# First four token blocks of a fused attention + gMLP kernel: loads re-split over two queues, a hand-set order on DVE and ACT

## The chip, the cores and the metric

One core of a Trainium2 chip. Times are device microseconds (us) of one execution; a lower time is better. "Span" is the time from the first to the last instruction in the profile; the device time is 1.7 to 2.5 us longer in nearly all runs here, in two clusters near 1.8 and 2.3, so for effects below a microsecond I compare spans as well. PE is TensorE, DVE is VectorE, ACT is ScalarE, POOL is GpSimd, SP is SyncE (which only issues transfers here).

## The reference

Two branches on the same layer-normed input, added to the residual (2048 tokens, width 512):

```python
xn = layernorm(x)                                   # 2048 x 512
A  = dilated_local_attention(xn @ wqkv) @ wo        # 32 heads, 8 keys, dilation 2
z  = gelu(xn @ w_in)                                # 2048 x 1792
z1, z2 = z[..., :896], layernorm(z[..., 896:])
B  = (z1 * (w_sp @ z2 + b_sp)) @ w_out              # w_sp is 2048 x 2048
return x + A + B
```

The tokens come in 16 blocks of 128. Block 0 to 3 must be loaded, normed and transposed before PE has any real work; the change is about them.

## The kernel before

The kernel is written as a list of tasks with reads, writes and estimated durations. A list scheduler turns them into one order per engine, and waits are put in from the dependencies. The order on PE is mostly the order of the code; on DVE, ACT and POOL the scheduler picks by its estimates. The loads at the start, in issue order:

```python
for h in range(2):                       # x block 0 in halves: x0a on SP, x0b on ACT
    dma(("sp", "act")[h], ... x2[0:128, 256*h : 256*h+256] ...)
ld_x(1, "sp")                            # x block 1, 128 KB
ld_win_h("w_in2a", FH, HF)               # first column half of z2's weights: 224 KB on each queue
ld_x(2, "sp")
ld_x(3, "act")
ld_win_h("w_in2b", FH + HF, HF)          # second column half: 224 KB on each queue
for which, eng in ((0, "sp"), (1, "act")):   # wq on SP, wk on ACT, 512 KB each
    ...
```

A block is normed with statistics on DVE, the power -0.5 on POOL, subtract and multiply on DVE, transposes on PE, an evacuation on ACT (block 0 half on ACT, half on DVE). Then z2 needs two half blocks of four matmuls each; the first half needs w_in2a only, the second w_in2b. Much later, at the end of the z2 stage, ACT alternates squares and gelus:

```python
def z2_n(j):
    for b in range(4 * j, 4 * j + 4):
        if b == NB - 2:
            z1_block(0)                  # four+four matmuls into two PSUM banks, then a gelu on ACT
        z2_sq(b)                         # square with row sum, on ACT
    z2_wave(j)
...
for b in range(1, NB):
    z1_block(b)
```

## Time and profile before

| | before |
|---|---|
| device time, median of the first 3 runs | 235.09 us (234.59 to 235.51) |
| span of the profiled run | 233.1 us |
| PE busy | 227.4 us, 98% |
| PE waits up to 217 us, once PE has real work | 0.86 us for w_in, 0.3 us for ACT at z1 |

The table of stretches of the kernel before, cut at the points where PE changes its work. Columns: start and end, length, then the busy time of PE, of its weight loads, of DVE, ACT and POOL with their instruction counts, the granted clock, the DMA share and GB/s:

```profile
5.19:8.26 3.07, 2.13 (x14) 0.95 (x15) 2.45 (x7) 1.43 (x4) 0.93 (x2) 1.00 1.04 353
8.26:14.37 6.11, 6.09 (x37) 3.30 (x38) 3.68 (x11) 4.75 (x15) 4.20 (x21) 1.00 1.05 339
80.46:107.37 26.91, 26.62 (x162) 14.93 (x160) 26.37 (x28) 17.90 (x25) 1.03 (x1) 1.00 0.25 52
107.37:217.60 110.23, 110.23 (x566) 55.21 (x565) 105.94 (x91) 45.37 (x76) 0.00 (x0) 1.00 0.85 196
```

The reader is to see that PE shows as idle for 0.94 us in the first stretch, 0.29 in the third (z1), and not at all in the 110 us of products after it. The change aims at the first and the third.

### The profile page before, as it was taken

To read this page: it belongs to the slowest core of one execution; us is meant where nothing else is said; L and a number is where in the kernel's file an instruction comes from. 1 tells how busy PE (TensorE), PEld (TensorE's weight loads), DVE (VectorE), ACT (ScalarE), POOL (GpSimd) and SP (SyncE) were. 2 spreads that over 40 slices of the span, in tenths; PEclk is the share of its full clock that TensorE was granted. 3 is DMA by queue.
4 is the path that set the end of the run, shared out by engine and by line. 5 is a ranking of instruction groups with operands and counts; after the bars stand their busy time and mean duration, and the time that the engine had idled before them with its cause. 6 is when DMAs were issued, how large, how long until landed. Compare 5 with 4: busy or idle time off the path is not lost.

```text
span 233.1 us, 3309 instructions
## 1 busy us (share of the span) xinstructions
PE 227.4 (98%) x1238; PEld 111.6 (48%) x1238; DVE 205.3 (88%) x238; ACT 129.4 (56%) x235; POOL 44.3 (19%) x74
## 2 busy tenths in 40 slices
PE   7899999999999999999999999999999999999995
PEld 2444444444444556555555554544544545545443
DVE  4688799989988899999999999999999999979910
ACT  3598768968889996556563243333423433255211
POOL 4455859257343101000000000000000000000000
PEclk9999999999999999999999999999999999999999
DMA  6997998941007200359709999999999747744082
GB/s 196 355 217 151 292 192 246 328 106 68 25 0 177 93 3 0 67 113 199 233 19 183 224 210 282 246 232 291 232 333 115 174 157 146 251 111 103 23 174 65
DMA packets 77456, 38.65 MB, mean 166 GB/s; under 512 B 65148, under 2 KB 75900, under 8 KB 76416
## 3 DMA queue, kind: packets, MB, share of 16 engines
q1 hardware_dynamic: 70272, 31.17, 58.9%
q10 hardware_dynamic: 6352, 5.15, 7.2%
q0 software_dynamic: 816, 2.12, 2.7%
q8 instruction: 10, 0.16, 0.3%
q14 instruction: 6, 0.05, 0.1%
HBM read 18.49 MB, written 4.21 MB: 97 GB/s over the span
## 4 chain that ended last, share of the span: by engine, by line
PE 88%; DMA 4%; ACT 3%; DVE 2%; SPq 1%; issue 0%; DVEq 0%
PE ps L1099 36%; PE ps L1218 13%; PE ps L757 12%; PE ps L886 10%; PE ps L904 8%; PE ps L737 6%; PE ps L796 3%; DMA arena<-in_B_w_in_dram 2%; DMA arena<-arena 2%; ACT arena L915 2%; ACT arena L910 1%; DVE arena L1176 1%; DVE arena L1116 1%; SPq L1179 1%; DVE arena L1132 0%; SPq L604 0%
## 5 line engine op out<-in xcount | busy, mean ns | idle before, releaser
L1099 PE MATMUL ps<-arena 128*128 128x448 bf16 x448 | 90.6, 352 | 0.0
L1099 PEld LDWEIGHTS ps<-arena 128*128 128x128 bf16 x448 | 43.8, 98 | 42.8 <-ACT arena L1055 0.3
L1218 PE MATMUL ps<-arena 128*128 128x512 bf16 (+2 forms) x187 | 44.1, 367 | 0.2 <-DMA arena<-arena 0.2
L1167 DVE TENSOR_TENSOR arena<-arena 128x4096 bf16<-128x4096 bf16 x16 | 36.6, 2286 | 0.3
L783 DVE TENSOR_TENSOR arena<-arena 128x4096 bf16<-128x4096 bf16 x16 | 36.0, 2280 | 0.0
L1176 DVE TENSOR_TENSOR arena<-arena 128x4096 bf16<-128x4096 bf16 (+2 forms) x24 | 33.6, 1401 | 1.1 <-DMA arena<-arena 0.4
L1055 ACT ACTIVATE arena<-ps 128x512 bf16<-128x512 f32 (+2 forms) x23 | 13.0, 564 | 34.8 <-PE ps L1099 23.8
L757 PE MATMUL ps<-arena 128*128 128x512 bf16 x128 | 28.5, 379 | 0.0
L1218 PEld LDWEIGHTS ps<-arena 128*128 128x128 bf16 x187 | 17.9, 98 | 18.9 <-DMA arena<-arena 0.5
L886 PE MATMUL ps<-arena 128*128 128x448 bf16 x128 | 25.7, 353 | 1.0 <-DMA arena<-in_B_w_in_dram 0.9
L904 PE MATMUL ps<-arena 128*128 128x448 bf16 x128 | 25.0, 353 | 0.3 <-ACT arena L910 0.3
L990 DVE TENSOR_TENSOR arena<-arena 128x1024 bf16<-128x1024 bf16 x32 | 21.1, 686 | 1.2 <-DMA arena<-in_B_w_sp_dram 0.9
L891 ACT ACTIVATE arena<-ps 128x448 bf16<-128x448 f32 x32 | 17.3, 546 | 5.1 <-PE ps L886 3.1
L757 PEld LDWEIGHTS ps<-arena 128*128 128x128 bf16 x128 | 12.4, 98 | 15.4 <-ACT arena L891 0.4
L765 ACT ACTIVATE arena<-ps 128x1024 bf16<-128x1024 f32 x16 | 16.3, 1020 | 5.8 <-PE ps L757 5.7
L904 PEld LDWEIGHTS ps<-arena 128*128 128x128 bf16 x128 | 14.3, 114 | 10.8 <-issue 0.8
L910 ACT ACTIVATE arena<-ps 128x896 bf16<-128x896 f32 x16 | 14.4, 914 | 8.9 <-PE ps L904 8.9
L886 PEld LDWEIGHTS ps<-arena 128*128 128x128 bf16 x128 | 12.1, 98 | 13.4 <-DMA arena<-in_B_w_in_dram 1.0
L771 POOL COPY arena<-arena 128x16 bf16<-128x16 bf16 x12 | 13.8, 1149 | 7.9 <-ACT arena L765 7.9
L915 ACT ACTIVATE arena<-arena 128x896 bf16<-128x896 bf16 x16 | 15.1, 944 | 0.2
L737 PE MATMUL ps<-arena 128*128 128x512 bf16 x64 | 14.5, 379 | 0.0
L1108 ACT ACTIVATE ps<-ps,fpool 128x448 f32<-128x448 f32 x16 | 9.7, 604 | 8.1 <-PE ps L1099 8.1
(74 smaller groups left out, 195.0 us busy)
## 6 DMA issues: line engine op xcount, KB each, us to landing
arena<-vscr SPq DMA_DIRECT2D x8, 1152.0 KB, 6.5
arena<-in_A_x_dram ACTq DMA_DIRECT2D x17, 128.0 KB, 3.9
vscr<-arena POOLq DMA_DIRECT2D x16, 128.0 KB, 2.9
arena<-in_A_x_dram SPq DMA_DIRECT2D x14, 128.0 KB, 6.2
out_dram<-arena ACTq DMA_DIRECT2D x14, 128.0 KB, 2.7
arena<-in_A_wqkv_dram SPq DMA_DIRECT2D x2, 512.0 KB, 7.8
arena<-in_B_w_in_dram SPq DMA_DIRECT2D x1, 896.0 KB, 6.0
arena<-in_B_w_out_dram SPq DMA_DIRECT2D x1, 896.0 KB, 5.7
```

What stands on the lines that cost most here:

```text
L737: last = t.matmul(bank(k), AC(off["xnT"] + dc * S + 128 * b, [[1, 128]]), AC(off["wv_raw"] + 512 * dc, [[1, 512]]), start=(dc == 0), stop= ...
L757: last = t.matmul(bank(k + which), AC(off["wqk"] + 1024 * dc + col0, [[1, 128]]), AC(off["xnT"] + dc * S + 512 * j, [[1, 512]]), start=(dc ...
L783: T("dve", lambda v: v.tensor_tensor(pbv, qb, kb, ALU.mult), reads=rd, writes=[("pb", s_)], est=c_dve(4096, 2.0), name="prod%d_%d" % (j, c ...
L886: last = t.matmul(ps[:, 512 * k: 512 * k + HF], AC(off["xnT"] + dc * S + 128 * b, [[1, 128]]), AC(off["w_in2"] + FH * dc + c0, [[1, HF]]), ...
L891: T("act", (lambda k, hf: lambda a: a.activation(A("z2", HF, FH * b + HF * hf), ps[:, 512 * k: 512 * k + HF], ACTF.Gelu_apprx_tanh, accum_ ...
L904: last = t.matmul(ps[:, 512 * (k + hf): 512 * (k + hf) + HF], AC(off["xnT"] + dc * S + t0, [[ts, 128]]), AC(off["w_in1"] + FH * dc + HF * ...
L915: T("act", lambda a: a.activation(A("sqj", FH), A("z2", FH, FH * b), ACTF.Square, accum_out=Fv("s2", 1, b)), reads=[("z2h", b, 0), ("z2h", ...
L990: T("dve", (lambda o_, x_, y_: lambda v: v.tensor_tensor(o_, x_, y_, ALU.subtract))(o_, x_, y_), reads=rd, writes=[wr], est=c_dve(NK * 128 ...
L1099: last = t.matmul(half(bk), lh(k), rh(k), start=(new and k == 0), stop=(k == NK - 1), skip_group_check=True)
L1167: T("dve", (lambda tv, iv, av: lambda v: v.tensor_tensor(tv, iv, av, ALU.mult))(tv, iv, av), reads=[("attn", j)] + ([("Ve", par)] if q < 2 ...
L1176: T("dve", (lambda o_, n: lambda v: v.tensor_tensor(o_, two(0, n), two(n, n), ALU.add))(o_, n), reads=[] if n > 512 else ["Vs", ("Ve", par ...
L1218: last = t.matmul(po, lh, rh, start=False, stop=(q == len(order) - 1), skip_group_check=True)
```

## The change

The intent: get w_in's second half to PE sooner, with the first two blocks of x in front in small pieces; have no engine do anything in the first 14 us but what PE waits for next; and, later, give PE a free bank pair sooner in the z1 stage. The diff, cut to its core (cuts are marked with dots; the comments on the order are mine):

```diff
-        for h in range(2):
-            dma(("sp", "act")[h], ... x2[0:128, 256 * h: 256 * h + 256] ...)
-        ld_x(1, "sp")
+        for b in range(2):
+            for h in range(2):
+                dma(("sp", "act")[h], ... x2[128 * b: 128 * b + 128, 256 * h: 256 * h + 256] ...)
         ld_win_h("w_in2a", FH, HF)
         ld_x(2, "sp")
+        ld_win_h("w_in2b", FH + HF, HF)
         ld_x(3, "act")
-        ld_win_h("w_in2b", FH + HF, HF)
-        for which, eng in ((0, "sp"), (1, "act")):
+        for which, eng in ((0, "sp"), (1, "sp")):
 ...
+            plan.sequence(dv)            # DVE: stats 0a 0b, aggr 0, stats 1a 1b, norm 0a 0b, aggr 1, evacuate 0b,
+                                         #   stats 2a, norm 1, stats 2b, aggr 2, stats 3, aggr 3, norm 2, norm 3
+            names = ["xTe0", "xTe1", "z2g0_0", "xTe2", "z2g0_1", "z2g1_0", "xTe3", "z2g1_1"]   # ACT
+            plan.sequence([named[n] for n in names])
 ...
         def z2_n(j):
-                if b == NB - 2:
-                    z1_block(0)
+                if b >= NB - 2:
+                    z1_block(b - NB + 2)
                 z2_sq(b)
 ...
-        for b in range(1, NB):
+        for b in range(2, NB):
             z1_block(b)
 ...
+        by_name["QKe3_3"].odeps.add(by_name["sexp1"])    # last evacuation of Q, K after the first exp
+        by_name["eV0_0"].odeps.add(by_name["sexp3"])     # first V evacuation of the products after the second exp
```

More of the change, by code (lines that the diff above doesn't have):

```diff
@@ L390, in build_kernel @@
     for name, n in (("mx", 128), ("Zb", 256), ("Z", 128), ("maskt", 128 if True else 256), ("st6", NB * 9),
-                    ("mv", NB * 2), ("st0", 15), ("rstd", NB), ("s1", 2 * NB), ("s2", NB), ("m2", NB), ("msq", NB),
+                    ("mv", NB * 2), ("st0", 45), ("rstd", NB), ("s1", 2 * NB), ("s2", NB), ("m2", NB), ("msq", NB),
                     ("vpe2", NB), ("rstd2", NB), ("mhalf", 4), ("bia", NB), ("bdf", NB // 2)):
@@ L462, in build_kernel @@
             if s_ < 2:
-                R1(("xin0", s_), "xin", 256, 256 * s_)
+                for h in range(2):
+                    R1(("xinh", s_, h), "xin", 256, 512 * s_ + 256 * h)
                 R1(("xn0", s_), "xn", 256, 256 * s_)
@@ L550, in build_kernel @@
           name="steps1")
-        T("dve", lambda v: v.memset(Fv("st0", 2, 12), 0.0), writes=["st0e"], est=160, name="steps2")
-        T("dve", lambda v: v.memset(Fv("st0", 1, 14), LN_EPS * D), writes=["st0e"], est=160, name="steps3")
+        T("dve", lambda v: v.memset(FCa(foff["st0"] + 12, [[15, 3], [1, 2]]), 0.0), writes=["st0e"], est=160, name="steps2")
+        T("dve", lambda v: v.memset(FCa(foff["st0"] + 14, [[15, 3], [1, 1]]), LN_EPS * D), writes=["st0e"], est=160, name="steps3")
         T("pool", lambda g: g.memset(mhalf, -0.5), writes=["mhalf"], est=110, name="mhalf")
@@ L617, in ld_win_h @@
                     256 * n * 2, (nm, h), writes=[(nm, h)], name="ld%s_%d" % (nm, h))
-        for h in range(2):
-            dma(("sp", "act")[h], (lambda h: lambda e: e.dma_start(A("xin", 256, 256 * h), x2[0:128, 256 * h: 256 * h + 256]))(h),
-                128 * 256 * 2, ("xin0", h), writes=[("xin0", h)], name="ldx0%s" % "ab"[h])
-        ld_x(1, "sp")
+        for b in range(2):
+            for h in range(2):
+                dma(("sp", "act")[h], (lambda b, h: lambda e: e.dma_start(
+                    A("xin", 256, 512 * b + 256 * h), x2[128 * b: 128 * b + 128, 256 * h: 256 * h + 256]))(b, h),
+                    128 * 256 * 2, ("xinh", b, h), writes=[("xinh", b, h)], name="ldx%d%s" % (b, "ab"[h]))
         ld_win_h("w_in2a", FH, HF)
         ld_x(2, "sp")
+        ld_win_h("w_in2b", FH + HF, HF)
         ld_x(3, "act")
-        ld_win_h("w_in2b", FH + HF, HF)
-        for which, eng in ((0, "sp"), (1, "act")):
+        for which, eng in ((0, "sp"), (1, "sp")):
             dma(eng, (lambda which: lambda e: e.dma_start(
@@ L664, in next_pair, with first_wave, bn, ag @@
             return k
-        def ln_first():
-            for h in range(2):
-                T("dve", (lambda h: lambda v: v.bn_stats(Fv("st0", 6, 6 * h), A("xin", 256, 256 * h)))(h),
-                  reads=[("xin0", h)], writes=[("st0", h)], est=420, name="bnst0%s" % "ab"[h])
-            T("dve", lambda v: v.bn_aggr(Fv("mv", 2), Fv("st0", 15)), reads=[("st0", 0), ("st0", 1), "st0e"],
-              writes=[("mv", 0)], est=180, name="bnag0")
-            T("pool", lambda g: g.tensor_tensor(Fv("rstd", 1), Fv("mv", 1, 1), Fv("mhalf", 1), ALU.pow),
-              reads=[("mv", 0), "mhalf"], writes=[("rstd", 0)], est=580, name="rstd0")
-            ks = (next_bank(), next_bank())
-            for h in range(2):
-                T("dve", (lambda h: lambda v: v.tensor_scalar(A("xn", 256, 256 * h), A("xin", 256, 256 * h), Fv("mv", 1),
-                                                              Fv("rstd", 1), ALU.subtract, ALU.mult))(h),
-                  reads=[("xin0", h), ("mv", 0), ("rstd", 0)], writes=[("xn0", h)], est=270, name="norm0%s" % "ab"[h])
-                def tr(t, h=h):
+        def first_wave():
+            dv = []
+            def bn(b, h):
+                dv.append(T("dve", lambda v: v.bn_stats(Fv("st0", 6, 15 * b + 6 * h), A("xin", 256, 512 * b + 256 * h)),
+                            reads=[("xinh", b, h) if b < 2 else ("xin", b)], writes=[("st0", b, h)], est=370,
+                            name="bnst%d%s" % (b, "ab"[h])))
+            def ag(b):
+                dv.append(T("dve", lambda v: v.bn_aggr(Fv("mv", 2, 2 * b), Fv("st0", 15, 15 * b) if b < 3 else Fv("st6", 9, 9 * b)),
+                            reads=[("st0", b, 0), ("st0", b, 1), "st0e"] if b < 3 else [("st6", b), "st_eps"],
+                            writes=[("mv", b)], est=200, name="bnag%d" % b))
+                T("pool", lambda g: g.tensor_tensor(Fv("rstd", 1, b), Fv("mv", 1, 2 * b + 1), Fv("mhalf", 1), ALU.pow),
+                  reads=[("mv", b), "mhalf"], writes=[("rstd", b)], est=580, name="rstd%d" % b)
+            def nm(b, c0=0, n=512, wr=None, tag=""):
+                dv.append(T("dve", lambda v: v.tensor_scalar(A("xn", n, 512 * b + c0), A("xin", n, 512 * b + c0), Fv("mv", 1, 2 * b),
+                                                             Fv("rstd", 1, b), ALU.subtract, ALU.mult),
+                            reads=[("xinh", b, h) for h in range(2)] + [("xin", b), ("mv", b), ("rstd", b)],
+                            writes=[wr or ("xn", b)], est=150 + n / 2, name="norm%d%s" % (b, tag)))
+            def xt(b, k, dcs, rd, tag=""):
+                def tr(t):
@@ L681, in tr @@
                     last = None
-                    for dc in (2 * h, 2 * h + 1):
-                        last = t.matmul(ps[:, 512 * ks[h] + 128 * dc: 512 * ks[h] + 128 * dc + 128],
-                                        A("xn", 128, 128 * dc), ident, start=True, stop=True)
-                    return last
-                T("pe", tr, reads=[("xn0", h), "ident"], writes=[("ps", ks[h])], est=2 * c_mm(128), name="xTr0%s" % "ab"[h])
+                    for dc in dcs:
+                        last = t.matmul(ps[:, 512 * k + 128 * dc: 512 * k + 128 * dc + 128],
+                                        A("xn", 128, 512 * b + 128 * dc), ident, start=True, stop=True)
@@ new lines, in tr, with ev @@
+                    return last
+                T("pe", tr, reads=[rd, "ident"], writes=[("ps", k)], est=len(dcs) * c_mm(128), name="xt%d%s" % (b, tag))
+            def ev(b, k):
+                T("act", lambda a: a.activation(AC(off["xnT"] + 128 * b, [[S, 4], [1, 128]]),
+                                                bank(k).rearrange("p (c n) -> p c n", c=4), ACTF.Copy),
+                  reads=[("ps", k)], writes=[("xnT", b)], est=c_act(512), name="xTe%d" % b)
+            bn(0, 0)
+            bn(0, 1)
@@ L687, in ln_first @@
+            ag(0)
+            bn(1, 0)
+            bn(1, 1)
+            k0, k1 = next_bank(), next_bank()
+            nm(0, 0, 256, ("xn0", 0), "a")
+            xt(0, k0, (0, 1), ("xn0", 0), "a")
             T("act", lambda a: a.activation(AC(off["xnT"], [[S, 2], [1, 128]]),
-                                            ps[:, 512 * ks[0]: 512 * ks[0] + 256].rearrange("p (c n) -> p c n", c=2),
+                                            ps[:, 512 * k0: 512 * k0 + 256].rearrange("p (c n) -> p c n", c=2),
@@ L689, in ln_first @@
                                             ACTF.Copy),
-              reads=[("ps", ks[0])], writes=["xnT0a"], est=c_act(256), name="xTe0")
-            T("dve", lambda v: v.tensor_copy(AC(off["xnT"] + 2 * S, [[S, 2], [1, 128]]),
-                                             ps[:, 512 * ks[1] + 256: 512 * ks[1] + 512].rearrange("p (c n) -> p c n", c=2)),
-              reads=[("ps", ks[1])], writes=["xnT0b"], est=c_dve(256), name="xTf0")
-            filler(cfg["fill0"], "fill0", 216.0 * cfg["fill0"], reads=("zeros", ("xn0", 1)))
+              reads=[("ps", k0)], writes=["xnT0a"], est=c_act(256), name="xTe0")
@@ new lines, in first_wave @@
+            nm(0, 256, 256, ("xn0", 1), "b")
+            xt(0, k1, (2, 3), ("xn0", 1), "b")
+            ag(1)
+            dv.append(T("dve", lambda v: v.tensor_copy(AC(off["xnT"] + 2 * S, [[S, 2], [1, 128]]),
+                                                       ps[:, 512 * k1 + 256: 512 * k1 + 512].rearrange("p (c n) -> p c n", c=2)),
+                        reads=[("ps", k1)], writes=["xnT0b"], est=c_dve(256), name="xTf0"))
+            filler(cfg["fill0"], "fill0", 216.0 * cfg["fill0"], reads=("zeros", ("xn0", 1)))
@@ new lines, in first_wave @@
+            z2_half(0, 0)
+            bn(2, 0)
+            nm(1)
+            k = next_bank()
+            xt(1, k, range(4), ("xn", 1))
+            ev(1, k)
+            bn(2, 1)
+            ag(2)
+            z2_half(0, 1)
+            dv.append(T("dve", lambda v: v.bn_stats(Fv("st6", 6, 27), A("xin", 512, 1536)), reads=[("xin", 3)],
+                        writes=[("st6", 3)], est=690, name="bnst3"))
+            ag(3)
+            nm(2)
+            z2_half(1, 0)
+            k = next_bank()
@@ new lines, in first_wave @@
+            xt(2, k, range(4), ("xn", 2))
+            ev(2, k)
+            z2_half(1, 1)
+            nm(3)
+            k = next_bank()
+            xt(3, k, range(4), ("xn", 3))
+            ev(3, k)
+            z2_half(2, 0)
+            z2_half(2, 1)
+            z2_half(3, 0)
+            z2_half(3, 1)
+            plan.sequence(dv)
+            names = ["xTe0", "xTe1", "z2g0_0", "xTe2", "z2g0_1", "z2g1_0", "xTe3", "z2g1_1"]
+            named = {t.name: t for t in plan.tasks if t.name in names}
@@ L696, in ln_block @@
+            plan.sequence([named[n] for n in names])
         def ln_block(b):
-            if b == 0:
-                return ln_first()
             sl = b % 4
@@ L702, in ln_block @@
             T("dve", lambda v: v.bn_stats(Fv("st6", 6, 9 * b), xin),
-              reads=[("xin", xs_)] + (["xnT0b"] if b == 2 else []), writes=[("st6", b)],
+              reads=[("xin", xs_)], writes=[("st6", b)],
               est=690, name="bnst%d" % b)
@@ L711, in ln_block @@
               reads=[("xin", xs_), ("mv", b), ("rstd", b)], writes=[("xn", sl)], est=400, name="norm%d" % b)
-            if b >= XDMA:
-                dma("sp", lambda e: e.dma_start_transpose(AC(off["xnT"] + 128 * b, [[S, 4], [1, 128]]),
-                                                          A("xn", 512, 512 * sl)),
-                    128 * 512 * 2, ("xT", sl), reads=[("xn", sl)], writes=[("xnT", b)], name="xTd%d" % b, xbar=True)
-                return
-            k = next_bank()
-            def tr(t):
-                last = None
-                for dc in range(4):
-                    last = t.matmul(ps[:, 512 * k + 128 * dc: 512 * k + 128 * dc + 128],
-                                    A("xn", 128, 512 * sl + 128 * dc), ident, start=True, stop=True)
-                return last
-            T("pe", tr, reads=[("xn", sl), "ident"], writes=[("ps", k)], est=4 * c_mm(128), name="xTr%d" % b)
-            T("act", lambda a: a.activation(AC(off["xnT"] + 128 * b, [[S, 4], [1, 128]]),
-                                            bank(k).rearrange("p (c n) -> p c n", c=4), ACTF.Copy),
-              reads=[("ps", k)], writes=[("xnT", b)], est=c_act(512), name="xTe%d" % b)
+            dma("sp", lambda e: e.dma_start_transpose(AC(off["xnT"] + 128 * b, [[S, 4], [1, 128]]),
+                                                      A("xn", 512, 512 * sl)),
+                128 * 512 * 2, ("xT", sl), reads=[("xn", sl)], writes=[("xnT", b)], name="xTd%d" % b, xbar=True)
         def v_block(b):
@@ L876, in softmax_tail, with z2_half, mm @@
               reads=[dk, "R"], writes=[("attn", j)], est=c_dve(1024, 2.0), name="sattn%d" % j, prio=FILL)
+        def z2_half(b, hf):
+            k = next_bank()
+            c0 = HF * hf
+            def mm(t):
+                last = None
+                for dc in range(4):
+                    last = t.matmul(ps[:, 512 * k: 512 * k + HF], AC(off["xnT"] + dc * S + 128 * b, [[1, 128]]),
+                                    AC(off["w_in2"] + FH * dc + c0, [[1, HF]]), start=(dc == 0), stop=(dc == 3))
+                return last
+            T("pe", mm, reads=[("xnT", b), (("w_in2a", "w_in2b")[hf], 0), (("w_in2a", "w_in2b")[hf], 1)], writes=[("ps", k)],
+              est=4 * c_mm(HF), name="z2_%d_%d" % (b, hf))
+            T("act", lambda a: a.activation(
+                A("z2", HF, FH * b + HF * hf), ps[:, 512 * k: 512 * k + HF], ACTF.Gelu_apprx_tanh,
+                accum_out=Fv("s1", 1, 2 * b + hf)),
+              reads=[("ps", k)], writes=[("z2h", b, hf), ("s1", b, hf)], est=c_act(HF, accum=True),
+              name="z2g%d_%d" % (b, hf), tbl="gelu")
         def z2_block(b):
             for hf in range(2):
-                k = next_bank()
-                c0 = HF * hf
-                def mm(t, k=k, c0=c0):
-                    last = None
-                    for dc in range(4):
-                        last = t.matmul(ps[:, 512 * k: 512 * k + HF], AC(off["xnT"] + dc * S + 128 * b, [[1, 128]]),
-                                        AC(off["w_in2"] + FH * dc + c0, [[1, HF]]), start=(dc == 0), stop=(dc == 3))
-                    return last
-                T("pe", mm, reads=[("xnT", b), (("w_in2a", "w_in2b")[hf], 0), (("w_in2a", "w_in2b")[hf], 1)], writes=[("ps", k)],
-                  est=4 * c_mm(HF), name="z2_%d_%d" % (b, hf))
-                T("act", (lambda k, hf: lambda a: a.activation(
-                    A("z2", HF, FH * b + HF * hf), ps[:, 512 * k: 512 * k + HF], ACTF.Gelu_apprx_tanh,
-                    accum_out=Fv("s1", 1, 2 * b + hf)))(k, hf),
-                  reads=[("ps", k)], writes=[("z2h", b, hf), ("s1", b, hf)], est=c_act(HF, accum=True),
-                  name="z2g%d_%d" % (b, hf), tbl="gelu")
+                z2_half(b, hf)
         def z1_block(b):
@@ L1020, in v_wave @@
                 v_block(b)
-        ln_wave(0)
+        first_wave()
         setup_masks()
-        z2_w(0)
         qk_wave(0)
@@ L1307, in build_kernel @@
             f_()
+        by_name = {t.name: t for t in plan.tasks}
+        by_name["QKe3_3"].odeps.add(by_name["sexp1"])
+        by_name["eV0_0"].odeps.add(by_name["sexp3"])
         plan.sequence(pe_seq)
```

## The prediction

> **What bounds the kernel now.** I read four views, in this order: the page (shares and slices), the chain that ended last, the table of stretches, and the timeline of the first 15 us. The page comes first because it says whether any engine but TensorE matters:
>
> ```profile
> PE 227.4 (98%) x1238; PEld 111.6 (48%) x1238; DVE 205.3 (88%) x238; ACT 129.4 (56%) x235; POOL 44.3 (19%) x74
> PE 88%; DMA 4%; ACT 3%; DVE 2%; SPq 1%; issue 0%; DVEq 0%
> ```
>
> TensorE (PE) has 5.7 us in the whole 233.1 us span in which it does nothing, and the chain that ended last runs 88% through it. So the change can only win from those 5.7 us, from PE work that is mere filler, or from work moved off PE; it moves none off. The chain in order of time says where it leaves PE:
>
> ```profile
> 2.70 5.52 DMA arena<-in_B_w_in_dram
> 8.22 0.05 issue
> 8.26 1.69 PE ps L886 x8
> ...
> 11.16 3.20 PE ps L886 x16
> 14.37 6.91 PE ps L757 x32
> ...
> 80.50 0.64 ACT arena L891 x2
> ...
> 85.96 0.81 ACT arena L910
> 86.77 0.05 issue
> 86.81 7.76 PE ps L904 x40
> ```
>
> The reader is to see three things. The chain starts with a load of w_in (the second column half's last piece, issued at 2.70, landed at 8.22), from there PE never lets go until 80.48; then comes an ACT (ScalarE) stretch to 86.77; the last exit is the tail after 217.6, which the change does not touch. Now the first stretch on PE itself, from the timeline of PE alone:
>
> ```profile
> 6.25 0.93 PE L886 MATMUL ps<-arena 128*128 128x448 bf16 x4
> 7.02 0.39 PE L722 MATMUL ps<-arena 128*128 128x128 bf16 x4
> 8.26 1.69 PE L886 MATMUL ps<-arena 128*128 128x448 bf16 x8 [0.86 <-DMA arena<-in_B_w_in_dram]
> ```
>
> The first half block of z2 (the gMLP gate input) runs at 6.25, the transposes of block 1 follow, then PE stands 0.86 us until the second half of w_in is there. After it PE is full: in the table of stretches PE is busy 5.92 of 5.94 us from 8.26 to 14.20, and all 30.80 us from there to 45.0. The only other PE wait up to 217 us in the view of waits is 0.3 us on ACT (the evacuation of z1) at 86.8.
>
> **What the Trainium skill says.** "Perfetto Trace Analysis", section "Optimization Strategy": find the gaps on the most contended engine and what blocks there. This trace agrees that this is the way to read it: two gaps in the first 217 us once PE has started on real work, 0.86 and 0.29 us. "DMA: Bandwidth & Descriptors", section "Queues, rings and completion order": each DMA engine takes turns between the queues that have work. The trace agrees: from 3.0 to 8.3 us the SP queue moved 0.16 + 0.14 + 0.14 + 0.18 + 0.24 = 0.86 MB and the ACT queue 0.24 + 0.12 + 0.20 + 0.15 + 0.25 = 0.96 MB, about half each. So a byte that goes ahead on one queue delays a later load of that queue by about two bytes' time. The same page, section "Issuing engines are not separate DMA queues": the second queue adds no bandwidth. The trace agrees: the windows from 4.3 to 11.3 us show 324 to 380 GB/s whether one queue or two carry it.
>
> **The change, part by part.**
>
> *Loads.* Before, w_in's last piece on SP had x0a (64 KB), x1 (128), w_in2a (224) and x2 (128) ahead of it: with itself 768 KB. After, x1 is split, so SP carries 64 + 64 + 224 + 128 + 224 = 704 KB up to the same piece. On ACT, w_in2b no longer stands behind x3: 64 + 64 + 224 + 224 = 576 KB in place of 640. With queues taking turns, 64 KB less on SP is 128 KB less over both, and at some 350 KB per us that is 0.37 us. Check on the kernel before: SP had moved 0.75 MB by 7.0 us, thus the 0.786 MB (768 KB) at about 7.2, and the load was seen at 8.22: a lag of 1.0 us. After, 0.72 MB is passed at about 6.85, so I expect w_in2b complete at **7.85 instead of 8.22**. The wk load goes from ACT to SP behind wq; both kernels have the same 2.4 MB ahead of the end of wk, so wq and wk land near 10.8 as now (8.0 and 7.7 us after issue at 2.73 and 3.18), 3 us before Q and K need them. Block 4 of x, too, has the same bytes before it (its statistics start at 11.20 after a DMA wait of 1.12).
>
> *Statistics of block 1 in two halves.* This adds one DVE instruction: a 256-column statistics pair took 0.75 us, a 512-column one 0.69. They sit between the aggregation of block 0 (ends 3.96) and rstd of block 0 on POOL (4.04 to 4.62), where DVE has nothing else. x1's halves were issued at the second place of each queue; x0's halves took 2.1 and 2.3 us to land, so the x1 halves should be there at about 3.6. Statistics then run 3.96 to 4.7, and the first normalisation starts at about 4.75 against 4.80. The first z2 matmul stays at about **6.2** (before 6.25): transposes, the two evacuations and the chain statistics, aggregation, rstd, norm are the same.
>
> *Order on DVE after that.* The hand-set order puts the first half of block 2's statistics ahead of block 1's norm. x2 was seen at 6.87 with 544 KB of its queue; now it is 480 KB, thus about 6.5. So norm 1 (0.41) goes from 6.18 to about 6.9, its transposes on PE from 7.02 to about 7.3, its evacuation on ACT ends at about 8.2. That is later than now, but it lies beside the wait for w_in2b and costs nothing as long as it is ready before 8.7, when the second block is due. Norm 2 comes at about 8.6 to 9.0 and norm 3 at 9.4 to 9.8; PE wants them at about 9.5 and 10.5. ACT backlogged takes a gelu every 0.52 us (11.69 to 12.20), PE needs 0.80 us for a half block (3.20 / 4), so ACT keeps up even with the order set on it.
>
> *PE after w_in2b.* Seven half blocks of 0.80 and two transposes of 0.22 (the chain's figures) are 6.04 us. 7.85 + 0.05 + 6.04 = 13.94 against 14.37 for the start of Q and K. The front thus gives **0.4 us**.
>
> *z1 block 1 inside the last square wave.* Now PE runs four z1 blocks and waits 0.29 us for a bank pair, because ACT does z1's gelu 1 only after the square of block 15 (0.94 + 0.19). With gelu 1 ahead of that square its bank comes free about 1 us earlier, and the wait goes: **0.3 us**. The square of block 15 and the norms of the last four z2 blocks come 0.9 us later; they now start at 89.14 and the sums built on them are needed by PE from about 109, so this has room.
>
> *The two order edges.* The third and last evacuation of Q and K after the second exp, and the first V evacuation after the last exp, are in the order that the trace has already (exp 70.52, evacuation 72.34; exp 116.89, evacuation 118.71). They hold it in place: 0.
>
> Sum: 0.4 + 0.3 = 0.7 us, so 235.09 - 0.7 = **234.4 us**. Would it all arrive at the end? The last merge on DVE waited 0.26 us for PE at 217.68, so DVE is near to taking over there. But DVE itself waits 1.26 us for ACT and PE at 205.08, so it too moves forward when PE does.
>
> **The rivals.** (a) *The gap closes wholly*: if w_in2b lands before 7.2 us, PE runs from 6.2 to about 13.3, and the front gives 1.05 us, in all 1.3: 233.8 us. For it: the four small x loads leave more of both queues to w_in. Against it: bytes ahead fall by 64 KB only, and the lag of 1.0 us from moved to seen stays. (b) *A new wait takes its place*: the fixed order lets a late x2 or x3 hold norm 1 or norm 2 and with it PE, which before could go on with whatever was ready. x3 is now last on ACT (704 KB, I estimate it at 7.6 against 5.6 now: 1.73 + 3.9). Half a microsecond of slack on norm 2 is all there is; if x3 comes at 8.5, PE loses 0.4 us and the front gives nothing: 234.8 us. (c) *The order elsewhere shifts*: the kernel's instruction order comes from a list scheduler fed with estimates, so other queue or DVE fill work may change places. DVE at 88%, with 16 to 32 tensor products of 2.3 us each, could then hold the final merge: plus or minus 0.5 us either way. (d) *DVE or the DMA is the hidden bound*, and PE's gain is given back at the end: 235.1. The 1.26 us wait at 205 speaks against it.
>
> **Range and chances.** Centre 234.4. Rival (a) with some luck in (c) gives 233.5; (b) with the spread of the runs before (234.59 to 235.51) gives 235.1. A 2% gain would be 4.7 us, almost all of PE's idle time including the start and the store at the end, which the change cannot touch. A 2% loss would need a new wait of 4.7 us, larger than all slack the order could miss by. So faster 0.01, same 0.98, slower 0.01.
>
> **What the profile of after would show.** Right: a PE wait for w_in of 0.3 to 0.6 us that ends at 7.7 to 8.0; Q and K start at 13.8 to 14.1; no PE wait on ACT near 86; DVE starts norm 1 at 6.7 to 7.0. Wrong: a PE wait between 8.7 and 14 with norm, x or the evacuation of the transposes as its releaser (rival b); the last merge on DVE without a wait for PE (rival d); the first z2 matmul off 6.2 by more than 0.2, which would mean that the x halves do not land as estimated.

## The result

The changed kernel: 234.22 us median of 6 runs (233.76 to 234.82), the kernel before 235.23 (234.59 to 235.51). The ratio is 0.9962 with a 95% interval of 0.9944 to 0.9981: within 2%, 0.9 us shorter. (A ratio here is the mean time of one kernel's fast runs over that of the other's of the same rounds, so not quite the ratio of the medians.) The predicted time was 234.4.

The profiled run is the fastest of the six: its span is 231.5 us, the six spans run up to 232.7 with a median of 231.9. What its profile shows is therefore the change at its best. The chain that ended last, in order of time (start, length, what):

```profile
2.70 4.71 DMA arena<-in_B_w_in_dram
7.42 0.05 issue
7.46 1.69 PE ps L926 x8
...
79.48 13.62 PE ps L948 x72
```

The load of w_in lands at 7.41 instead of 8.22, and z1 (L948) runs 72 matmuls in a row: the ACT stretch from 80.50 to 86.77 has left the chain. PE's own timeline for the start:

```profile
6.12 0.93 PE L926 MATMUL ps<-arena 128*128 128x448 bf16 x4
7.01 0.40 PE L693 MATMUL ps<-arena 128*128 128x128 bf16 x4
7.46 1.69 PE L926 MATMUL ps<-arena 128*128 128x448 bf16 x8
```

No line has a wait at its end any more. The same stretches as before, cut at the same events:

```profile
5.07:7.46 2.39, 2.25 (x15) 1.00 (x14) 1.77 (x6) 0.40 (x2) 0.57 (x1) 1.00 1.09 378
7.46:13.43 5.97, 5.92 (x36) 3.27 (x38) 3.80 (x11) 5.13 (x17) 4.13 (x21) 1.00 1.10 354
79.48:105.89 26.41, 26.41 (x161) 15.02 (x160) 25.83 (x30) 17.77 (x27) 1.03 (x1) 1.00 0.27 56
105.89:216.12 110.23, 109.81 (x559) 55.22 (x565) 106.17 (x91) 45.45 (x77) 0.00 (x0) 1.00 0.85 195
```

The lengths answer the question where the time went, for this pair of runs: up to w_in's second half 8.26 - 7.46 = 0.80, the rest of the first wave 6.11 - 5.97 = 0.14, z1 26.91 - 26.41 = 0.50, the products 0.00, and 0.12 in the tail. With 0.04 in between that is 1.6 us, the difference of the two spans. (16 matmul records are missing from the second trace. So PE's busy time there is too low, and if the first record of Q and K is among the missing, 13.43 is one matmul late; the 0.14 and the 0.04 are best read together, as 0.18 between the start of w_in's second half and z1.)

But 1.6 is not the 1.0 of the medians. Some of this pair is luck, and the experiments must say which part.

### The profile page after: what moved, and what is told of

It reads as the page before. It is cut to its first block, busy times and chain, and to the rows that moved or that the text cites. A ratio compares the mean times of both kernels' runs of the same rounds, so it can differ in the third digit from the quotient of the medians.

```text
span 231.5 us, 3297 instructions
## 1 busy us (share of the span) xinstructions
PE 226.4 (98%) x1222; PEld 111.8 (48%) x1238; DVE 205.4 (89%) x240; ACT 128.4 (55%) x235; POOL 38.2 (17%) x74
## 4 chain that ended last, share of the span: by engine, by line
PE 91%; DMA 4%; DVE 2%; SPq 1%; issue 1%; ACT 0%; DVEq 0%
PE ps L1142 36%; PE ps L1261 13%; PE ps L798 12%; PE ps L948 11%; PE ps L926 10%; PE ps L778 6%; PE ps L837 3%; DMA arena<-in_B_w_in_dram 2%; DMA arena<-arena 2%; DVE arena L1219 1%; DVE arena L1159 1%; SPq L1222 1%; DVE arena L1175 0%; SPq L622 0%; SPq L605 0%
## 5 line engine op out<-in xcount | busy, mean ns | idle before, releaser
L1261 PE MATMUL ps<-arena 128*128 128x512 bf16 (+2 forms) x178 | 42.3, 366 | 0.6
L798 PE MATMUL ps<-arena 128*128 128x512 bf16 x124 | 27.9, 379 | 0.3 <-issue 0.2
L948 PE MATMUL ps<-arena 128*128 128x448 bf16 x128 | 24.8, 353 | 0.0
L948 PEld LDWEIGHTS ps<-arena 128*128 128x128 bf16 x128 | 14.4, 114 | 10.2 <-issue 0.8
L778 PE MATMUL ps<-arena 128*128 128x512 bf16 x61 | 14.2, 379 | 0.3 <-issue 0.2
L1098 ACT ACTIVATE ps<-arena 128x512 f32<-128x512 bf16 (+2 forms) x17 | 9.7, 574 | 6.4 <-ACT arena L1098 4.7
```

Of the source, the lines that this page charges most:

```text
L778: last = t.matmul(bank(k), AC(off["xnT"] + dc * S + 128 * b, [[1, 128]]), AC(off["wv_raw"] + 512 * dc, [[1, 512]]), start=(dc == 0), stop= ...
L798: last = t.matmul(bank(k + which), AC(off["wqk"] + 1024 * dc + col0, [[1, 128]]), AC(off["xnT"] + dc * S + 512 * j, [[1, 512]]), start=(dc ...
L948: last = t.matmul(ps[:, 512 * (k + hf): 512 * (k + hf) + HF], AC(off["xnT"] + dc * S + t0, [[ts, 128]]), AC(off["w_in1"] + FH * dc + HF * ...
L1098: T("act", lambda a: a.activation(out_, in_, ACTF.Copy), reads=reads, writes=writes, est=c_act(n), name=name)
L1261: last = t.matmul(po, lh, rh, start=False, stop=(q == len(order) - 1), skip_group_check=True)
```

## The experiments

Because a list scheduler sets the order, undoing one part of the change would reorder hundreds of later instructions. So in all experiments but one I recorded each engine's order from its base kernel and replayed it, with only the named moves made. Line numbers in their profiles differ for that reason. All gave correct results. Twelve runs in four groups; each group shared one chip and its runs of the kernel before.

**loads_only.** The kernel before in its own order, with the new loads.

```diff
-SP:  x0a x1 w_in2a x2 w_in2b wq        ACT: x0b w_in2a x3 w_in2b wk
+SP:  x0a x1a w_in2a x2 w_in2b wq wk    ACT: x0b x1b w_in2a w_in2b x3
```

> The kernel before with its recorded instruction order on every engine, and only the new loads (x1 in halves on both queues, the second half of w_in ahead of x3, wk on SP). Theory A, the front's gain is the loads: w_in's last piece lands at 7.4 to 7.6 us instead of 8.2, Q and K start at 13.4 to 13.7 instead of 14.37, the PE wait of 0.3 us at z1 stays, and the time is 0.8 us under before (ratio 0.9965). Theory B, the gain is the hand-set order on DVE, ACT and PE: a new PE wait for norm 1 or its evacuation takes the place of the wait for w_in, Q and K start at 14.2 or later, ratio 1.000.

234.94 us, ratio 0.9976 (0.9949 to 1.0004). w_in landed at 7.76, Q and K started at 13.97, the z1 wait stayed at 0.3. The direction is theory A's, the size is half of it or less: the median span is 232.9 against 233.0.

**order_only.** The changed kernel in its own order, with the old loads (the diff above, reversed).

> The changed kernel with its recorded order on every engine, and only the old loads back. Theory A: PE waits for w_in to about 8.2 us as before, Q and K start at 14.2 to 14.4, no PE wait at z1, and the time is 0.3 to 0.5 us under before (ratio 0.9983). Theory B: PE finds other work and Q and K start before 13.8; ratio 0.9965 or less.

234.76 us, ratio 0.9976 (0.9947 to 1.0004). w_in landed at 8.25, Q and K started at 14.27: the hand-set order does not close the wait for w_in, and theory B falls. The median span is 232.5 against 233.0, which is the z1 part.

But the order does win something at the front, which the start of Q and K, shown a matmul late by a missing record, hides. PE around the transposes of block 3, first in the kernel before, then in order_only:

```profile
10.77 0.39 PE L722 MATMUL ps<-arena 128*128 128x128 bf16 x4
11.16 3.20 PE L886 MATMUL ps<-arena 128*128 128x448 bf16 x16
```

```profile
10.80 0.39 PE L770 MATMUL ps<-arena 128*128 128x128 bf16 x4
11.03 3.19 PE L1003 MATMUL ps<-arena 128*128 128x448 bf16 x16
```

From the transposes to the next half block it is 0.39 us, then 0.23. In the kernel before, ACT evacuates block 2's transposes only at 10.52, behind two gelus, and PE's weight load waits for it (0.18 us on PEld; the line of PE shows none). The hand-set order puts that evacuation ahead of both gelus. From PE's start on w_in's second half to its first z1 matmul it is 72.03 or 72.04 us in the four traces with the order of the kernel before (before, replay_before, loads_only, z1_only) and 71.84 to 71.86 in the eight with the hand-set order and no new wait in that stretch: **0.19 us**, whatever the loads did.

**z1_only** and **no_z1.** One pair of ACT instructions exchanged in the kernel before, and exchanged back in the changed kernel.

```diff
 ACT (z1_only):  ... square 14
-  square 15, gelu z1_1
+  gelu z1_1, square 15
```

> The kernel before with one pair of ACT instructions exchanged: the gelu of z1 block 1 ahead of the square of z2 block 15. Theory A: the PE wait of 0.29 us near 86.8 goes and the time falls by 0.3 us (ratio 0.9987); the first product stage starts at about 107.0 instead of 107.37. Theory B, the later norms of z2 give it back: the first product stage starts earlier but DVE makes PE or the last merge wait later; ratio 1.000.

> The changed kernel with that pair of ACT instructions put back (square of block 15 first). Theory A: a PE wait of 0.3 us near 85.5 comes back and the time is 0.3 to 0.5 us over the changed kernel, so about 0.6 us under before (ratio 0.9975). Theory B: no change against the changed kernel (ratio 0.9962 to before).

Times: 235.59 us, ratio 1.0002 (0.9973 to 1.0031), and 234.92 us, ratio 0.999 (0.996 to 1.002). The whole-run times disappoint for z1_only, and so do its six spans, 232.8 to 233.8 with a median of 233.3 against 233.0. Its profile shows where: in that run w_in's last piece landed at 8.85 instead of 8.22, with the same loads in the same order, and Q and K started at 15.12. The stage itself did what theory A says. From PE's first z1 matmul to its first product it took 81.01 to 107.42 = 26.41 us in z1_only and 80.14 to 107.04 = 26.90 us in no_z1. no_z1 missed its expected ratio of 0.9975, so I repeated it beside a control later.

**replay_before, replay_after, no_z1_again.** The two kernels replayed without any move, as controls, and no_z1 once more on the same chip.

> Control: the kernel before, its recorded order replayed, nothing changed. Theory A (a replay is the same program): span within 0.2 us of before, Q and K start at 14.2 to 14.5, ratio 1.000. Theory C (each build has its own luck with the front's loads, as z1_only's late w_in at 8.85 us suggests): the spans of its six runs lie together but off before's by 0.3 us or more.

> Control: the changed kernel, its recorded order replayed, nothing changed. Theory A: the median span is 231.9 as in the six runs of the changed kernel, Q and K start between 13.4 and 14.2, 92.5 us from there to the first product stage, ratio 0.996. Theory C: the median span is 232.3 or more.

> The changed kernel with the two ACT instructions put back, once more beside its own control. Theory A: 93.0 us from the start of Q and K to the first product stage as in the first run, against 92.5 in the control; the median span is 0.5 us over that of the control on the same chip. Theory B: less than 0.2 us.

| run | time, us | ratio to before | median span | w_in landed | z1 to products |
|---|---|---|---|---|---|
| replay_before | 235.29 | 0.9975 (0.9949 to 1.0001) | 233.0 | 8.28 | 26.90 |
| replay_after | 234.81 | 0.9953 (0.9928 to 0.9978) | 232.5 | 8.01 | 26.41 |
| no_z1_again | 234.89 | 0.9958 (0.993 to 0.9985) | 233.1 | 8.43 | 26.90 |

The replay of the kernel before is the same program, and its ratio is 0.9975 all the same. A ratio in these groups can thus be off by a quarter of a per cent, 0.6 us, which is more than one part of this change is worth; spans and stages within a trace say more.

PE's timeline of the z1 stage, first of no_z1_again, then of replay_after:

```profile
80.41 6.22 PE L1026 MATMUL ps<-arena 128*128 128x448 bf16 x32
86.92 7.76 PE L1026 MATMUL ps<-arena 128*128 128x448 bf16 x40 [0.30 <-ACT arena L1032]
```

```profile
79.99 13.78 PE L1026 MATMUL ps<-arena 128*128 128x448 bf16 x72
```

The same 72 matmuls take 86.92 + 7.76 - 80.41 = 14.27 us with the wait and 13.78 without: 0.49 us, though the wait is shown as 0.30. In every one of the thirteen traces with this order of stages the stretch from z1 to the products is 26.90 or 26.91 us with the square first and 26.41 or 26.42 with the gelu first, whatever the front did. This part of the change is settled: **0.49 us**. The span difference of the pair, 0.6, agrees.

The loads are not so tidy. The controls differ by 0.5 us in span and in time on one chip, no more than the z1 stage (0.49) and the hand-set order (0.19) account for. Theory C, a fixed offset for each build, stays open. For it: replay_after's median span of 232.5 meets its figure (232.3 or more) and not the 231.9 of theory A, and z1_only's six spans are late together (its z1 stage alone should have put them 0.49 below). Against it: replay_before agrees with the kernel before, and w_in's landing differs between two runs of one program as well (no_z1: 8.16, then 8.43 on another chip). With the new loads it landed at 7.41, 7.76, 7.96, 8.01, 8.16 and 8.43 us (the six traces with all of the change's loads, that of no_edge below among them; mean 7.96), with the old ones at 8.22, 8.25, 8.85 and 8.28 (mean 8.40). The middle values are 7.99 and 8.27, 0.28 apart. Median spans without the z1 part say less: loads_only 232.9 against 233.0, no_z1 233.05 against 233.0, no_z1_again 233.1 against 233.2, and in the last two the order's 0.19 is still to be taken off. The headline's medians leave 1.0 - 0.49 - 0.19 = 0.3. So the loads gain **between -0.2 and 0.3 us** in a typical run, which is not shown to differ from nothing, and 0.8 in a lucky one.

**Why so little? wk_act, x1_whole.** The traces with the new loads have one thing in common that I had not foreseen. Stretch 3 to 4 us of the kernel before, then of the changed kernel, the last two columns being the DMA share and GB/s:

```profile
3.00:4.00 1.00, 1.00 (x4) 0.40 (x3) 0.92 (x3) 0.74 (x1) 0.00 (x0) 1.00 1.02 315
```

```profile
3.00:4.00 1.00, 1.00 (x4) 0.39 (x3) 0.96 (x5) 0.73 (x1) 0.15 (x1) 1.00 0.72 141
```

The DMA engines run half empty there. In all eight traces with four 64 KB loads in front the rate is 77 to 184 GB/s; in the four with the old loads it is 274 to 340. In that microsecond this pair differs by 0.17 MB; but the new loads moved more before it, so by 4 us the changed kernel is 0.10 MB behind, worth 0.3 us at some 350 GB/s, about the 0.37 us that the bytes moved back should win. By 7 us this run has caught up (1.54 MB against 1.52); the control has not (1.43 in replay_after, 1.48 in replay_before). Over the six traces the landing roughly follows the depth of the lull: 141 and 155 GB/s go with 7.41 and 7.76, 121 and 107 with 7.96 and 8.01, 77 with 8.16, but 123 with 8.43. Two experiments: one gives wk back to ACT (to see whether the empty ACT queue matters), one gives up the halving of x1.

```diff
 wk_act:    SP:  x0a x1a w_in2a x2 w_in2b wq [-wk-]   ACT: x0b x1b w_in2a w_in2b x3 {+wk+}
 x1_whole:  SP:  x0a [-x1a-] {+x1+} w_in2a x2 w_in2b wq wk   ACT: x0b [-x1b-] w_in2a w_in2b x3
```

> The changed kernel with wk back on the ACT queue, behind x3; all else in the recorded order. Theory A (bytes ahead on each queue decide): w_in's last piece has the same bytes ahead on SP and as many on ACT, landing unchanged within 0.1 us, Q and K start as in the control. Theory D (the SP queue's last piece gains because the ACT queue runs empty behind x3 and leaves it the engines): w_in lands 0.4 us later than in the control, and Q and K start 0.3 to 0.5 us later.

> The changed kernel with x1 as one load on SP again (ACT: x0b, w_in2a, w_in2b, x3); all else in the recorded order. The runs so far with four 64 KB loads ahead show the DMA engines at only 77 to 184 GB/s from 3 to 4 us, the kernel before 291. Theory E (the four small loads are issued too slowly to keep the engines fed, and this lull eats the bytes saved): 3 to 4 us moves over 250 GB/s, w_in's last piece lands at 7.5 to 7.8 us, 0.2 to 0.4 earlier than the 8.0 of the replayed control, and the median span is 232.2 or less. Rival (bytes ahead on SP decide, 768 KB in place of 704): it lands at 8.2 to 8.4 and the median span is 232.7 or more.

wk_act: 234.09 us, ratio 0.9921 (0.9896 to 0.9947), w_in landed at 7.93 against 8.01 in the control. Theory D's 0.4 us later does not show: the queue that carries wk seems not to matter for w_in, as far as one trace can say. Its median span is 232.05 against the control's 232.5 on the same chip, which I had not expected and can't explain from its one trace; that stays open.

x1_whole: 234.55 us, ratio 0.997 (0.9937 to 1.0004), median span 232.2 against before's 233.2. The stretch of 3 to 4 us in its trace:

```profile
3.00:4.00 1.00, 1.00 (x4) 0.38 (x3) 0.94 (x3) 1.00 (x1) 0.00 (x0) 1.00 1.03 260
```

The lull is gone with one load made whole, so the small loads cause it: shown. Why they do is worked out, not shown: an issue slot of SP is 0.44 us in these traces (0.87 us for two), 64 KB per slot on each of two queues is about 300 GB/s, and 64 KB are moved in 0.19 us at 350 GB/s; the w_in loads stand a slot later on ACT and the engines run dry before their data comes. What the lull costs is not shown: w_in's last piece landed at 7.94, behind theory E's 7.5 to 7.8, ahead of its rival's 8.2 to 8.4, and only 0.07 before the control's 8.01. The 64 KB that stand ahead of it again on SP and the lull seem to be worth about the same, so halving x1 bought nothing that can be seen. And a new wait took the place of the old. PE's timeline of x1_whole:

```profile
6.49 0.92 PE L1005 MATMUL ps<-arena 128*128 128x448 bf16 x4
8.12 0.40 PE L772 MATMUL ps<-arena 128*128 128x128 bf16 x4 [0.71 <-DVE arena L763]
8.35 1.78 PE L1005 MATMUL ps<-arena 128*128 128x448 bf16 x8
```

PE's printed wait is no longer for w_in but for norm 1 (L763, on DVE), because the hand-set order puts block 2's statistics ahead of norm 1 and x2 came only at 7.3. This is rival (b) of the prediction: the order on ACT gains, the order on DVE can lose. It also shows in no_z1_again (0.28 us ahead of the transposes of block 1), hidden there behind a w_in that came later still.

**w2_norm.** The changed kernel with w_in2b ahead of x2 on SP, and norm 1 ahead of block 2's statistics.

```diff
-SP:  ... w_in2a x2 w_in2b ...       DVE: ... stats 2a, norm 1, stats 2b ...
+SP:  ... w_in2a w_in2b x2 ...       DVE: ... norm 1, stats 2a, stats 2b ...
```

> The changed kernel with the second half of w_in ahead of x2 on SP, and norm 1 ahead of block 2's statistics on DVE. Two bytes' time for each byte ahead: 128 KB less ahead of w_in's last piece brings it 0.7 us forward, to 7.3 us, and PE runs on from the first half block without a wait for w_in; norm 2 must then be ready by about 9.5. Theory A: no PE wait over 0.2 us up to Q and K, which start at 13.3 to 13.5; median span 231.8. Rival b (a new wait): PE waits for norm 2, since x2 lands near 7.4, and the span stays at 232.3 or more.

234.62 us, ratio 0.9974 (0.9945 to 1.0004), median span 232.6. PE's second half block started at 7.62 without a wait for w_in, so in this one trace the bytes do what they should: 128 KB less ahead brought w_in at least 0.4 us forward against the control (0.7 was expected). Then PE waited 0.66 us for norm 2 ahead of the transposes of block 2 at 10.07, as x2 came only at 7.9. Q and K started at 14.31: rival (b) again, nothing won.

**x1_norm.** A try at a version that beats both: x1 whole, and norm 1 first.

> A try at a version that beats both: x1 as one load on SP (no lull of the DMA engines from 3 to 4 us) and, as well, norm 1 ahead of block 2's statistics on DVE, so that it no longer waits for x2. Theory: the DVE wait of 1.1 us ahead of norm 1 in x1_whole goes, the transposes of block 1 run by 7.4, w_in's last piece then ends the front's only PE wait at 7.5 to 7.8, Q and K start at 13.5 to 13.8 instead of 14.2, median span 231.9 against 232.2 in x1_whole. Rival: x2's statistics now come later and PE waits for norm 2 near 9.5, Q and K start at 14.1 or later and the span stays at 232.2.

234.14 us, ratio 0.9927 (0.9902 to 0.9952), median span 232.15 against before's 233.3 on its chip. 305 GB/s from 3 to 4 us, w_in landed at 7.78, Q and K started at 13.59, and the front's only wait on PE once it has real work is

```profile
7.83 1.69 PE L1005 MATMUL ps<-arena 128*128 128x448 bf16 x8 [0.26 <-DMA arena<-in_B_w_in_dram]
```

It beats the kernel before. Against the changed kernel its interval overlaps that of the headline (0.9944 to 0.9981) and that of the replayed control, so I call it probably, not surely, better; the same holds for wk_act.

**no_edge.** The changed kernel without the two order edges, scheduled anew.

```diff
-        by_name["QKe3_3"].odeps.add(by_name["sexp1"])
-        by_name["eV0_0"].odeps.add(by_name["sexp3"])
```

> The changed kernel without its two order edges, ordered anew by its scheduler, which then puts the first exp behind the z1 evacuations and the two reductions of the last Q and K wave after 40 products. If the edges only hold the trace's order (my prediction, 0): the front and the stage from Q and K to the products take what they take in the control within 0.2 us, ratio to before 0.9953. Rival (the edges carry part of the gain): DVE gets the softmax late and the last merge or PE waits for it; 0.5 us or more slower than the control.

260.28 us, ratio 1.1064 (1.1033 to 1.1096): 25 us slower than the kernel before. The rival holds, far beyond the half microsecond I gave it. The busy tenths on its page, one digit for each 6.5 us:

```profile
PE   8999999999999999920699999099999999999975
...
DVE  4687989989959880019699998995998999999920
...
PEclk9999999999999999995599999659999999999999
```

and its waits, of PE and of DVE (line waiting, what it waited for, us in total, times, longest):

```profile
PE ps L837 <- DVE arena L857: 13.4, 1, 13.4
PE ps L1142 <- DVE arena L1034: 6.5, 1, 6.5
```

```profile
DVE arena L884 <- ACT arena L874: 19.1, 1, 19.1
```

The scheduler, fed with slightly other start times, put the first exp (L874) behind the z1 gelus: its table load starts at 112.5 us instead of 68.5. DVE, at 88% of the kernel before the second fullest engine, then stands 19.1 us for the exp's result (L884 sums it), PE waits 13.4 us for a reduction bank that DVE must free, and the clock granted to PE falls in its two gaps, to five or six tenths, 0.954 in the mean of the run. DVE's 19 us are never made up. The two edges were removed together, so the run does not say what each is worth.

## Why the prediction was right or wrong

*Time and range.* 234.4 predicted, 234.22 measured, in the range; the change is within 2%. That the number is so close is partly luck: the two terms of the sum, 0.4 and 0.3, were mis-sized in opposite directions, and the 0.19 us of the order on ACT were not in it.

*Loads, "0.37 us".* In the middle of the scatter the landing held: w_in's last piece was to land at 7.85, the traces with the new loads have 7.41 to 8.43 with a middle of 7.99. The gain did not: it is between -0.2 and 0.3 us in a typical run. The step that did not hold is "at some 350 KB per us": it took the engines for full from 3 us on, and the four small loads leave them at 77 to 184 GB/s for a microsecond. That this is what shrank the gain is argued from the bytes, not shown: with the lull gone w_in came at 7.94 and 7.78 (x1_whole, x1_norm), inside the scatter. Rival (a), w_in early enough to close the gap, is what the headline's profiled run happens to show (no PE wait, Q and K at 13.43): one trace in six.

*PE after w_in's second half, "6.04 us" in both.* The prediction read "busy 5.92 of 5.94 us" as a full engine. A stop of 0.17 us for ACT was hidden in it, and the order set on ACT, from which the prediction expected only no harm ("ACT keeps up"), removes it: the stretch up to z1 is 0.19 us shorter.

*z1, "0.3 us".* The mechanism was right, the size was taken from the wait that the profile prints. The stage gained 0.49. The reason can be read off: one 448-column matmul is shown as 352 ns long while a running stream starts one every 6.05 / 32 = 189 ns. The shown wait begins when the last matmul's modelled end is past, so the stop costs PE up to 352 - 189 = 163 ns more than is printed: 0.30 + 0.16 = 0.46 of the 0.49. The same 0.16 is what hid the stop for ACT in the first wave. The Trainium skill has both durations, in "TensorE: Matmul & The Clock Gate", sections "Single matmul latency" ((398 + N) / 2.4, 352 ns for 448 columns) and "Back-to-back issue gap" (N / 2.4 + 2.5, 189 ns, for what the page calls an isolated gap). This trace has both numbers; its 352 is itself a modelled end, so only the 189 is a measurement that agrees.

*First z2 matmul at 6.2.* 6.12 in the headline run. Statistics of block 1 were to run 3.96 to 4.7 with the halves there by 3.6; they ran 3.68 to 4.37. (The change adds two DVE instructions and not one, since block 2's statistics are halved too.) In other runs z2 started between 6.1 and 6.7; in the latest of them, no_z1_again, PE waited 0.72 us for w_in2a, which the prediction did not have.

*Norm 1 "to about 6.9", beside the wait for w_in.* 6.56 to 7.45, as x2 came; hidden as said, as long as w_in is later. Rival (b) is real, but bites only when w_in comes sooner (x1_whole, w2_norm).

*The order edges, "0".* Against the kernel before this is right: the order is the same as there. But rival (c) gave the scheduler's whims "plus or minus 0.5 us", and without the edges they cost 25 us. The edges are no part of the gain; they are what kept the rest from being a loss.

*The end.* The last merge on DVE waited 0.19 us for PE (0.26 before), and the products take 110.23 us in both, so what PE gains reaches the end. Rival (d) falls.

*What stays open.* Why w_in's landing scatters by up to a microsecond with the same loads, whether a build has an offset of its own, what the loads are worth in the median, and whether wk_act's 0.45 us over the control is more than that scatter.

## What to carry to other kernels

Size a stall by how much later the same work ends, not by the wait that the profile prints: here a stop printed as 0.30 us on PE cost 0.49. When loads are cut small to get the first one sooner, look at the DMA rate just behind them: here they left the engines at 77 to 184 GB/s for a microsecond, and no gain of the loads stood clear of the scatter. A nearly full busy share does not mean that a pipelined engine never stops; compare the length of the same work in two orders. And where a scheduler with estimates sets the order, freeze it before you compare parts, and pin the one or two orders that a whole engine hangs on; here two pins, removed together, were worth 25 us while the change they came with was worth one.

## What the Trainium skill lacked or had wrong

- "DMA: Bandwidth & Descriptors", section "Issuing engines are not separate DMA queues", calls the issue time saved by a second queue "usually small relative to the DMA itself". The start of this kernel is a case where it isn't: a slot of 0.44 us issues 64 KB, which would move in 0.19 us at 350 GB/s (an estimate), and the rate behind four such loads was 77 to 184 GB/s against 260 to 340 without.
- The same page has no word on how far the landing of one load scatters between runs of one kernel: 8.16 and 8.43 us for the same program, 8.22 and 8.85 for the same loads in the same order.
- "Perfetto Trace Analysis", section "Optimization Strategy", has the reader find gaps between slices. It doesn't say that a gap on PE shows less than it costs: 0.30 us printed, 0.49 us lost; a stop of 0.17 us was not printed on PE at all. (The page does say elsewhere that the end of a matmul in a profile is an estimate.)
- "TensorE: Matmul & The Clock Gate", section "Back-to-back issue gap", gives 131 ns per matmul as the sustained rate at N=512 and says that N / 2.4 + 2.5 over-counts there. In this kernel 32 such matmuls take 6.91 us in the chain, 216 ns each, which is the formula (215.8) and not 131. (An earlier part of the same page has 215.7 as measured, so the page disagrees with itself.)
